# Two record scatters in every chunk of the attention, in a kernel of pooled attention and a noisy top-2 mixture of experts

## The chip, the cores and the metric

One Trainium2 chip, one of its cores. The metric is the device time of one execution in microseconds (us); the kernel before takes 1044.02 us, the median of 3 runs (1043.8 to 1044.55).

The engines are named as in the profile: PE multiplies matrices (PEld is its weight load), DVE works on vectors, ACT evaluates functions, POOL is the general engine that here issues all indirect DMAs, SP issues the plain ones.

## The reference

```python
# attention: q, k, v of 8 batches x 8 heads x 576 tokens x 64
k_p, v_p = mean of k, v over groups of 8 tokens             # 72 pooled keys
attn = softmax(q @ k_p.T / 8)
x = (attn @ v_p) as 4608 tokens x 512
# mixture of 8 experts, 512 -> 1024 -> 512
noisy = x @ w_gate + log1p(exp(x @ w_noise)) * noise
top2 of noisy; weights = softmax over the two
out[token] = sum over its two experts of weight * (relu(x @ w1[e]) @ w2[e])
```

## The kernel before, in words

The attention is cut into four pairs of batches (pr 0 to 3), and a pair into nine chunks of 128 tokens (ci 0 to 8): four units of kind D give two chunks each (jj 0 and 1), one unit of kind R gives a single one, at ci 4. So there are 36 chunks, numbered i = 9 pr + ci. A chunk runs through the letters of an order string: "0", "1" and "2" are the scores (`qk`) of a third of the heads of the next unit, with the exponentials on ACT; "e" transposes a chunk's exponentials; "v" is the product with the pooled values (`av`, of the chunk before), whose division by the row sums DVE writes to xr (L419); "b" runs background work, "x" calls `adv`.

The gate's logits come out of `av` too. When all nine chunks of a pair have them, `route` works out for the pair's 1152 tokens the two experts, the weights and the place in each expert's list. It is a generator, and `advance(n, m)` takes n of its steps in each chunk at "x". Its first steps add up the logits over the heads, for pairs 0 and 1 on POOL (L509, L510), first for eight chunks and then for the last one; DVE goes on from there (L517). Its last steps build a record of four 32-bit words for each token and expert (rec, last word at L635) and put 18 closures on the list `scq`: one indirect DMA each that scatters 128 records to their places in rec_dram (L638). Behind those of pair 1 they put the load of the first group's records (`load_recs`, L679) and its row gathers (`fetch`, L706); behind those of pair 2 the same for the second group; behind those of pair 3 for the third group and for all other experts.

The second argument m of `advance` says how many entries of `scq` are issued then. They are in POOL's queue in that order, and a scatter also waits (pace) for an instruction of the attention of its moment: at "0", "1" and "2" for the last exponential, at "x" for the last product of DVE. `quiet` is 0 in the first chunk of pairs 1 and 2 and the last chunk of pair 1, and 1 elsewhere in the pairs that have something to issue. What is left on `scq` after the last chunk is issued in the first stage of the MoE, by `hook1` with the numbers of POPS for each of the eight steps f, and by `hook` in its second stage.

The MoE takes the rows of each expert in three groups of tiles of 128 rows. Expert 0's first group (4 tiles) is gathered in the attention, and its transposes (L756) stand in the last two chunks. Group by group PE runs stage 1 (L1017: 8 x 12 matmuls) and stage 2 (L1128, 24 matmuls a tile; L1094 where three tiles are joined). The transposes of the second group (2 tiles) stand in PE's order behind the second tile of the first group's stage 2, those of the third (4 tiles) behind the first tile of the second group's. Groups of the other experts come by row gathers (L715) and a copy through DRAM by SP (L720, L723).

Of the kernel before, what the change touches and what calls it, by code (L numbers as in the profile page):

```python
# [19 lines left out]
def kernel(  # L20
# [25 lines left out]
    NP = B // 2  # L46
    NCH = 9
# [92 lines left out]
    STEPS = (2, 2, 2, 2)  # L140
# [193 lines left out]
    def qtr(u, half, hp=None):  # L334
        kind, pr, b, jp = u
        if half == 0:
            QTT[u] = ap_.tile([P, H, P], F32, tag="qT", name=f"qT{pr}_{b}_{jp}", bufs=2)
        elif kind == "R":
            return
        qT = QTT[u]  # L340
        qp = ps2.tile([P, 4, P], F32, tag="one", name=f"qp{pr}_{b}_{jp}_{half}", bufs=2)
        for i in range(4):
            if kind == "R":
                src = QR[pr][:, 2 * i:2 * i + 2]
            else:
                src = QT[b][:, half * 4 + i, 2 * jp:2 * jp + 2]
            nc.tensor.transpose(qp[:, i], src.rearrange("p a d -> p (a d)"), ident)  # L347
        with tc.high_priority(offset=HP if hp is None else hp):
            nc.scalar.copy(qT[:, half * 4:half * 4 + 4], qp)
# [35 lines left out]
    def et(u, jj):  # L385
        kind, pr, b, jp = u
        nm = f"{pr}_{b}_{jp}_{jj}"
        ex = EX[u][:, jj]
        eT = ap_.tile([P, NEB, P], F32, tag="eT", name=f"eT{nm}", bufs=2)
        for n0, n1 in EG:  # L390
            ep = ps2.tile([P, 512], F32, tag="one", name=f"ep{nm}_{n0}", bufs=2)
            for n in range(n0, n1):
                nc.tensor.transpose(ep[:BST, (n - n0) * P:(n - n0 + 1) * P], ex[:, ES[n]:ES[n] + BST], ident)  # L393
            with tc.high_priority(offset=HP):
                (nc.vector.tensor_copy if n0 and EV >> jj & 1 else nc.scalar.copy)(eT[:BST, n0:n1].rearrange("p n t -> p (n t)"), ep[:BST, :(n1 - n0) * P])  # L395
        return eT
# [50 lines left out]
    def wload():  # L447
        if not pieces:
            return
        e, i, h = pieces.pop(0)  # L450
        st = wp.tile([P, DF], F32, tag="wst", name=f"wst{e}_{i}_{h}", bufs=WS)
        if i < 2:
            src = moe_w1[e].rearrange("(p c) f -> p c f", p=P)[:, 2 * i + h]
            dst = st
        else:
            r0 = (i - 2) * 4 * P + h * 2 * P
            src = moe_w2[e, r0:r0 + 2 * P, :].rearrange("(c p) f -> p c f", p=P)
            dst = st.rearrange("p (c f) -> p c f", c=2)
        nc.sync.dma_start(dst, src)
        staged.append(st)  # L460
# [26 lines left out]
    def drain(g):  # L487
        for _ in g:
            pass
# [255 lines left out]
    def rows_of(grp, psum):  # L745
        e, t0, nt = grp
        xh = wp.tile([P, NDB, 4 * P], F32R, tag="q", name=f"xh{e}_{t0}", bufs=2)
        xl = wp.tile([P, NDB, 4 * P], F32R, tag="q", name=f"xl{e}_{t0}", bufs=2)
        XT[grp] = (xh, xl)
        for t in range(nt):  # L750
            xg = XG.pop((e, t0 + t))
            if e == 0:
                xp = psum(f"xp{t0 + t}").rearrange("p (b c) -> p b c", b=NDB)
                xv = xg.rearrange("p (c b) -> p b c", b=NDB)
                for db in range(NDB):
                    nc.tensor.transpose(xp[:, db], xv[:, db], ident)  # L756
                nr = 2 if t0 + t == 9 else 4
                xT = xp.rearrange("p b (r j) -> p b r j", j=32)[:, :, :nr]
            else:
                nr = 2 if t0 + t == 9 else 4  # L760
                xt = pools[0].tile([P, 4, NDB, 32], F32, tag="xt", name=f"xt{e}_{t0 + t}", bufs=2)
                nc.vector.transpose(xt[:, :nr], xg[:, :nr * P].rearrange("p (r i b) -> p r b i", i=32, b=NDB))
                xT = xt.rearrange("p r b j -> p b r j")[:, :, :nr]
            cs = slice(t * P, t * P + nr * 32)
            xhv = xh[:, :, cs].rearrange("p b (r j) -> p b r j", j=32)
            xlv = xl[:, :, cs].rearrange("p b (r j) -> p b r j", j=32)
            SP_[0] = (nc.scalar.copy(xhv, xT), nc.vector.tensor_sub(xlv, xT, xhv.bitcast(F32)))  # L767
            yield
# [13 lines left out]
    def advance(n, m):  # L782
        for _ in range(n):
            while gens:
                try:
                    next(gens[0])
                    break
                except StopIteration:
                    gens.pop(0)
        for _ in range(min(m, len(scq))):  # L790
            scq.pop(0)()
# [84 lines left out]
    for i, (ui, u, jj) in enumerate(chunks):  # L876
        pr, ci = divmod(i, NCH)
        if ci == 0:
            lgs[pr] = (rp if pr % 2 else ap_).tile([P, NCH, H, 2 * E], F32, tag="lg", name=f"lg{pr}")
        single = u[0] == "R"  # L880
        has = ui + 1 < NU
        if single:
            order = OR
        else:
            order = OD[jj]
        eT = None
        quiet = 0 if ci == 0 and pr <= NP // 2 or ci == NCH - 1 and pr < NP // 2 else 1

        def bgs():
            for f in bg.get(i, ()):  # L890
                f()

        def adv():
            pace[0] = lastx[0]
            advance(STEPS[pr], 2 * quiet if pr >= NP // 2 else quiet)

        for o in order + ("" if "b" in order else "b") + ("" if "x" in order else "x"):
            if o == "v" and i == 0:
                drain(pg[0])
            if o == "b":  # L900
                bgs()
            elif o == "x":
                adv()
            elif o == "e":
                eT = et(u, jj)
            elif o == "v":
                if due:
                    due.pop()()
                if ci == NCH - 1 and pr < NP - 1:
                    gens.append(route(pr, 0, NCH, lgs[pr], one))  # L910
                elif ci == NCH - 1:
                    rt = route(pr, 0, NCH, lgs[pr], lambda nm: mone(nm))
                    next(rt)
                due.append(lambda u=u, jj=jj, ci=ci, eT=eT, lg=lgs[pr]: av(u, jj, ci, eT, lg))
            elif o in "012":
                if has:
                    qk(units[ui + 1], int(o))
                    if pr and (o == "0" or not single):
                        pace[0] = lasta[0]
                        advance(0, quiet)  # L920
            elif ui + 2 < NU:
                qtr(units[ui + 2], "qr".index(o))
        if i == 24:
            for _ in range(WS):
                wload()
        if i == 33:
            splits = rows_of(groups[0], one)
        if pr == 3 and ci:
            with tc.issue_after(lastl[0].ins), tc.issue_after(lasta[0].ins):
                next(first[0], None) if ci < 5 else next(first[1], None)  # L930
        if ci == 4 and pr >= HS:
            gens.append(route(pr, 0, 5, lgs[pr], one))
# [206 lines left out]
    def mone(name):  # L1139
        return bank()  # L1140
# [10 lines left out]
                    wgens.pop(0)  # L1151

    s0 = SP_[0]
    POPS = {0: (8, 0, 0, 2, 3, 3, 3, 3), 1: (100, 0, 0, 0, 0, 0, 0, 0)}

    def hook1(i, f):
        if i == 0 and f == 0:
# [2 lines left out]
        elif i == 0:  # L1160
            next(rt, None)
            next(rt, None)
        advance(0, POPS[i][f])

# [151 lines left out]
```

## Time and profile before

| what | value |
|---|---|
| median of 3 runs | 1044.02 us |
| span of the profiled execution (its own time, from its first to its last instruction) | 1041.8 us |
| PE busy | 995.3 us, 96% |
| POOL busy | 371.0 us, 36% |
| record scatters, L638 | 72, 76.2 us |

The span is that of one execution taken by the hardware profiler. Busy times are shares of that span; an engine that is idle costs time only where the end of the program waits for it. The profile shows the granted clock of PE (PEclk, as a share of full speed) by stretches.

### The profile page before, as it was taken

The numbers are of one execution on the slowest core, as the hardware profiler recorded it, in microseconds if no ns is written. First come the engines' busy times: TensorE is split into PE (matmuls) and PEld (weight loads), VectorE is DVE, ScalarE is ACT, GpSimd is POOL, SyncE is SP. The second block draws the span as 40 slices with busy tenths as digits, with TensorE's granted clock in tenths as the row PEclk, the third lists the DMA queues.
The fourth block names the chain that finished last, engine by engine and source line by source line (L and its number), as shares of the span: only waits on it lengthen the run. The fifth ranks groups of instructions, "written<-read, shape, count | busy, mean of one in ns | idle before, by whom it ended". The sixth has DMA issues, their size and how long they took to land.

```text
span 1041.8 us, 16452 instructions
## 1 busy us (share of the span) xinstructions
PE 995.3 (96%) x5832; PEld 889.2 (85%) x5832; DVE 549.0 (53%) x1277; ACT 345.5 (33%) x857; POOL 371.0 (36%) x419
## 2 busy tenths in 40 slices
PE   7998989699999999999999999999999999999996
PEld 5897878587998898888988898889888988898995
DVE  5798768494343554554445445444554455456242
ACT  5786667541123122321232123212321232124120
POOL 4024462537310433154215421542154215421514
PEclk9999989799999999999999999999999999999999
DMA  9997853244615656577348736773577357844624
GB/s 277 336 305 235 274 155 103 82 138 118 181 60 144 211 191 191 144 242 219 111 131 249 233 120 170 249 227 100 151 248 245 116 142 258 249 137 142 203 88 136
DMA packets 137382, 190.36 MB, mean 183 GB/s; under 512 B 29155, under 2 KB 84084, under 8 KB 137274
## 3 DMA queue, kind: packets, MB, share of 16 engines
q1 hardware_dynamic: 111834, 121.84, 38.8%
q0 software_dynamic: 25440, 67.05, 20.6%
q8 instruction: 72, 1.18, 0.5%
q14 instruction: 36, 0.29, 0.1%
HBM read 126.07 MB, written 70.74 MB: 189 GB/s over the span
## 4 chain that ended last, share of the span: by engine, by line
PE 88%; issue 3%; ACT 2%; DVE 1%; DMA 1%; POOL 1%; another core or an unknown queue 1%; SPq 1%; POOLq 0%; DVEq 0%; ACTq 0%
PE bank L1017 37%; PE bank L1128 27%; PE bank L1094 10%; PE a L408 5%; PE s L375 3%; PE ep L393 2%; PE qp L347 2%; ACT ex L382 1%; DMA v<-in_v_dram 1%; ACT eT L395 1%; POOL out_dram L1073 1%; PE kT L298 0%; PE vr L325 0%; SPq L219 0%
## 5 line engine op out<-in xcount | busy, mean ns | idle before, releaser
L1017 PE MATMUL bank<-xh,w 128*128 128x512 f32 (+6 forms) x1536 | 390.4, 338 | 0.6 <-issue 0.6
L1017 PEld LDWEIGHTS bank<-xh,w 128*128 128x128 f32 x1536 | 270.3, 188 | 21.4 <-issue 0.9
L1128 PE MATMUL bank<-w,hh 128*128 128x512 f32 x880 | 271.7, 390 | 1.3 <-issue 1.2
L1017 PE MATMUL bank<-xl,w 128*128 128x512 f32 (+6 forms) x768 | 259.7, 338 | 1.2 <-issue 0.9
L1028 ACT ACTIVATE hh<-bank 128x512 fp32r<-128x512 f32 (+4 forms) x192 | 96.7, 510 | 459.9 <-PE bank L1017 369.2
L1029 DVE SCALAR_TENSOR_TENSOR hl<-bank,hh 128x512 fp32r<-128x512 f32 (+4 forms) x192 | 110.1, 579 | 243.1 <-ACT hh L1028 212.7
L1128 PEld LDWEIGHTS bank<-w,hh 128*128 128x128 f32 x880 | 164.8, 188 | 34.8 <-issue 1.1
L1128 PE MATMUL bank<-w,hl 128*128 128x512 f32 x440 | 171.4, 390 | 1.0 <-issue 1.0
L1017 PEld LDWEIGHTS bank<-xl,w 128*128 128x128 f32 x768 | 144.6, 188 | 11.3 <-DVE xl L767 0.6
L1065 DVE SCALAR_TENSOR_TENSOR pv<-bank,raw,pv 128x128 f32<-128x128 f32 x196 | 55.5, 342 | 111.8 <-DMA pv<-slot_dram,raw 51.8
L1069 POOL DMA_DIRECT2D slot_dram<-yt x17 | 9.8, 576 | 276.0 <-DVE yt L1065 225.5
L638 POOL DMA_INDIRECT rec_dram<-rec,pos x72 | 76.2, 1058 | 85.3 <-DVE rec L635 26.9
L1094 PE MATMUL bank<-hh,w 128*128 128x240 f32 (+3 forms) x512 | 103.6, 298 | 2.2 <-issue 1.7
L1128 PEld LDWEIGHTS bank<-w,hl 128*128 128x128 f32 x440 | 82.6, 188 | 19.5 <-issue 2.4
L1049 POOL DMA_INDIRECT pv<-slot_dram,raw x70 | 68.7, 982 | 62.4 <-DMA slot_dram<-ys 34.2
L481 DVE TENSOR_TENSOR w<-wst,w 128x512 fp32r<-128x512 f32 x128 | 82.6, 682 | 11.1 <-ACT w L480 10.6
L1094 PEld LDWEIGHTS bank<-hh,w 128*128 128x128 f32 x512 | 82.6, 189 | 2.7 <-issue 2.1
L480 ACT CAST w<-wst 128x512 fp32r<-128x512 f32 x128 | 73.0, 618 | 27.1 <-DMA wst<-in_moe_w_dram 27.1
L715 POOL DMA_INDIRECT row<-x_dram,raw x70 | 70.2, 1004 | 21.3 <-issue 20.7
L1069 POOL DMA_DIRECT2D slot_dram<-pv x55 | 31.7, 576 | 125.1 <-DVE pv L1065 89.2
L1094 PE MATMUL bank<-hl,w 128*128 128x320 f32 (+3 forms) x256 | 76.0, 297 | 0.0
L382 ACT ACTIVATE ex<-s,mx 128x72 f32<-128x72 f32 x288 | 70.8, 342 | 12.8 <-DVE mx L380 7.5
(165 smaller groups left out, 1032.3 us busy)
## 6 DMA issues: line engine op xcount, KB each, us to landing
wst<-in_moe_w_dram SPq DMA_DIRECT2D x64, 512.0 KB
via<-row SPq DMA_DIRECT2D x266, 64.0 KB
xg<-via SPq DMA_DIRECT2D x63, 256.0 KB
slot_dram<-pv POOLq DMA_DIRECT2D x55, 256.0 KB
k<-in_k_dram SPq DMA_DIRECT2D x7, 1280.0 KB
v<-in_v_dram SPq DMA_DIRECT2D x16, 512.0 KB
x_dram<-xr SPq DMA_DIRECT2D x16, 512.0 KB
q<-in_q_dram SPq DMA_DIRECT2D x7, 1024.0 KB
```

Source lines behind the costliest of these rows:

```text
L382: lasta[0] = nc.scalar.activation(ex[:, jj, EPOS[h] * G:(EPOS[h] + 1) * G], sv[:, i], AF.Exp, bias=mx[:, i:i + 1])
L480: nc.scalar.copy(hv, sv)
L481: nc.vector.tensor_sub(lv, sv, hv.bitcast(F32))
L638: s = nc.gpsimd.indirect_dma_start(out=rec_dram[:, :], out_offset=bass.IndirectOffsetOnAxis(ap=pos[:, i, c:c + 1], axis=0), in_=rec[:, c, ...
L715: turn_of("pool", lambda: nc.gpsimd.indirect_dma_start(out=row[:32 * nr], out_offset=None, in_=x_dram[:, :], in_offset=bass.IndirectOffset ...
L1017: nc.tensor.matmul(part(ph), w1s(e, a, db, f), part(xs[b][:, db]), start=(i == 0), stop=(i == 3 * NDB - 1))
L1028: act = nc.scalar.activation(hh[:, :n], ph[:, :n], AF.Relu)
L1029: last = nc.vector.scalar_tensor_tensor(hl[:, :n], ph[:, :n], 0.0, hh[:, :n].bitcast(F32), op0=OP.max, op1=OP.subtract)
L1049: turn_of("pool", lambda: nc.gpsimd.indirect_dma_start(out=pv[:np_], out_offset=None, in_=slot_dram[:P + e * CAP, :], in_offset=bass.Indir ...
L1065: nc.vector.scalar_tensor_tensor(r_, y_, wc, pv[:plain] if plain else r_, op0=OP.mult, op1=OP.add)
L1094: nc.tensor.matmul(part(py), w2s(e, b, f)[:, mb * P:(mb + 1) * P], part(hs[f][a]), start=(i == 0), stop=(i == 3 * NFB - 1))
L1128: mm = nc.tensor.matmul(py, hs[f][a][:, cs], w2s(e, b, f), start=(i == 0), stop=(i == 3 * NFB - 1))
```

## The change

The number of entries of `scq` issued in a chunk no longer depends on the pair or on `quiet`, which goes away. From pair 1 on, one is issued behind the first scores of a chunk (at "0" for the first chunk of a unit and the single one, at "2" for the second chunk of a unit), and in every chunk one at "x". Nothing is issued at "1". The last two chunks have no scores of a next unit and issue only the one at "x". At the first step of the MoE all that is left is issued (100 in place of 8).

```diff
-        quiet = 0 if ci == 0 and pr <= NP // 2 or ci == NCH - 1 and pr < NP // 2 else 1
-
         def bgs():
             for f in bg.get(i, ()):
                 f()
 
         def adv():
             pace[0] = lastx[0]
-            advance(STEPS[pr], 2 * quiet if pr >= NP // 2 else quiet)
+            advance(STEPS[pr], 1)
...
-                    if pr and (o == "0" or not single):
+                    if pr and (o == "0" or o == "2" and not single):
                         pace[0] = lasta[0]
-                        advance(0, quiet)
+                        advance(0, 1)
...
-    POPS = {0: (8, 0, 0, 2, 3, 3, 3, 3), 1: (100, 0, 0, 0, 0, 0, 0, 0)}
+    POPS = {0: (100, 0, 0, 2, 3, 3, 3, 3), 1: (100, 0, 0, 0, 0, 0, 0, 0)}
```

## Rows read from the trace of the kernel before

**Rows 1.** The page: busy time of each engine; the group of the scatters.

```profile
PE 995.3 (96%) x5832; PEld 889.2 (85%) x5832; DVE 549.0 (53%) x1277; ACT 345.5 (33%) x857; POOL 371.0 (36%) x419
...
L638 POOL DMA_INDIRECT rec_dram<-rec,pos x72 | 76.2, 1058 | 85.3 <-DVE rec L635 26.9
```

**Rows 2.** Stretches: length, busy us of PE, PEld, DVE, ACT, POOL (instructions), PEclk, DMA.

```profile
88.54:102.49 13.95, 11.32 (x86) 9.69 (x84) 10.18 (x20) 9.74 (x33) 9.92 (x9) 1.00 0.71 177
102.49:115.23 12.74, 12.72 (x99) 12.28 (x100) 10.32 (x27) 9.79 (x33) 6.03 (x8) 0.87 0.77 236
115.23:124.74 9.51, 8.24 (x85) 7.39 (x80) 6.97 (x27) 7.01 (x26) 5.39 (x5) 1.00 0.91 312
124.74:135.35 10.61, 10.00 (x90) 8.08 (x88) 8.69 (x44) 6.34 (x23) 2.29 (x4) 1.00 0.66 208
135.35:161.81 26.46, 22.09 (x140) 20.27 (x141) 15.68 (x35) 15.97 (x54) 19.51 (x18) 0.81 0.45 131
161.81:186.22 24.41, 22.11 (x199) 18.74 (x198) 20.46 (x90) 18.16 (x62) 4.74 (x6) 1.00 0.39 131
186.22:204.21 17.99, 7.66 (x57) 7.07 (x56) 5.21 (x15) 7.31 (x26) 11.71 (x12) 0.74 0.18 46
204.21:213.59 9.38, 8.72 (x49) 8.07 (x48) 7.80 (x19) 4.63 (x9) 4.75 (x6) 0.78 0.57 155
```

**Rows 3.** The chain of waits in order of time: start, length, what.

```profile
195.22 7.78 another core or an unknown queue
```

**Rows 4.** POOL in order of time: start, length, instruction [idle before, releaser].

```profile
135.21 0.97 POOL L638 DMA_INDIRECT rec_dram<-rec,pos  x1 [7.71 <-DVE rec L635]
...
161.11 0.97 POOL L638 DMA_INDIRECT rec_dram<-rec,pos  x1 [0.30 <-issue]
163.49 0.59 POOL L679 DMA_DIRECT2D raw<-rec_dram  x1 [1.42 <-DMA rec_dram<-rec,pos]
...
186.52 1.00 POOL L638 DMA_INDIRECT rec_dram<-rec,pos  x1 [15.79 <-DVE rec L635]
...
200.62 0.96 POOL L638 DMA_INDIRECT rec_dram<-rec,pos  x1 [0.30 <-issue]
```

**Rows 5.** PE and ACT in order of time, near the longest holes.

```profile
194.64 0.42 PE L393 MATMUL ep<-ident,ex 128*112 128x128 f32 x1 [2.50 <-remote]
...
203.03 0.59 ACT L395 COPY eT<-ep 112x512 f32<-112x512 f32 x1 [7.80 <-remote]
...
203.66 1.98 PE L756 MATMUL xp<-ident,xg 128*128 128x128 f32 x8 [7.83 <-ACT eT L395]
```

**Rows 6.** POOL and DVE in order of time, route of pair 1 and chunk 30.

```profile
112.75 0.89 POOL L509 TENSOR_TENSOR lg<-lg 128x64 f32<-128x64 f32 x2 [0.40 <-DVE lg L421]
...
113.98 0.23 DVE L517 SCALAR_TENSOR_TENSOR rt<-rt 128x72 f32<-128x72 f32 x1 [0.47 <-POOL rt L510]
...
177.09 0.68 DVE L419 TENSOR_TENSOR xr<-a,rd 128x512 f32<-128x512 f32 x1
```

**Rows 7.** POOL and SP in order of time, a row gather and its copy.

```profile
271.54 1.01 POOL L715 DMA_INDIRECT row<-x_dram,raw  x1 [0.31 <-issue]
...
274.99 8.24 SPq L720 DMA_DIRECT2D via<-row  x16
```

**Rows 8.** POOL in order of time, at the start of the MoE.

```profile
223.31 0.58 POOL L679 DMA_DIRECT2D raw<-rec_dram  x1 [1.42 <-DMA rec_dram<-rec,pos]
226.93 1.36 POOL L706 DMA_INDIRECT xg<-x_dram,raw  x1 [3.04 <-DMA raw<-rec_dram]
...
233.00 1.18 POOL L638 DMA_INDIRECT rec_dram<-rec,pos  x1 [3.44 <-DVE rec L635]
...
262.17 1.01 POOL L706 DMA_INDIRECT xg<-x_dram,raw  x1 [4.31 <-DMA raw<-rec_dram]
```

**Rows 9.** The chain of waits in order of time, the MoE's first groups.

```profile
245.99 0.96 PE bank L756 x8
...
278.01 1.92 PE bank L756 x16
```

## The prediction

> **What bounds the kernel now.** I read the page first: PE is busy for 96% of the span and POOL, which issues the 72 record scatters (76.2 us), for 36% [rows 1]. So POOL's own time buys nothing, and the question is where PE is not busy. Outside the attention there is hardly such a place, so the second view is the table of stretches from the first record scatter to the first MoE matmul [rows 2]. The reader is to see two kinds of stretch in it. In three of them POOL issues scatters back to back (88.54 to 102.49, 135.35 to 161.81, 186.22 to 204.21: 58.40 us together), and PE is idle for 2.63 + 4.37 + 10.33 = 17.33 us, 29.7%. In the other five (66.65 us) PE is idle for 0.02 + 1.27 + 0.61 + 2.30 + 0.66 = 4.86 us, 7.3%. The longest single hole is in the chain too: 7.78 us from 195.22 whose releaser the profile can't name [rows 3]. Third, POOL in order of time says why the scatters lie so [rows 4]: the route of pair 1 was to hand its records out from chunk 21 on, but its record words come from DVE only at 135.2, by when several chunks' worth is queued; a scatter takes 0.97 us and the next can follow 0.30 us later, and all 18 go in one run, the last at 161.11. Pair 2's start at 186.52 after a wait of 15.79 us and run on to 200.62. Fourth, PE's idle time in the third run: 2.50 us before 194.64, without a releaser, and 7.83 us before 203.66, put down to an ACT copy that itself had waited 7.80 us for something unnamed [rows 5]. No row names a scatter as the cause; only the coincidence does.
>
> **The change part by part.** The profiled execution has a span of 1041.8 us and the median of the runs is 1044.02, so 2.2 us lie around the span; I make the sum on the span and add them.
>
> *The scatters themselves.* 72 before, 72 after; no instruction is added on PE, DVE or ACT. Counting pops: before, a chunk of pair 1 takes 2 or 3, of pairs 2 and 3 takes 3 or 4, and chunks 17 and 18 none. After, each takes 2 (the last two chunks 1 each). Pair 0's scatters then end in chunk 21 in place of 20, pair 1's in chunk 30 in place of 26, and of pair 2's 18 only 7 are issued in the attention in place of 16.
>
> *What spreading buys.* The nearest rows for a chunk with two scatters are 115.23 to 124.74 (5 in 9.51 us) and 204.21 to 213.59 (4 in 9.38 us): idle 1.27 + 0.66 = 1.93 us of 18.89, 10.2% [rows 2]. PE's busy time in the eight stretches is 102.86 us. At 10.2% idle throughout they take 102.86 / 0.898 = 114.5 us in place of 125.05: 10.5 us less. Not all runs go: a route that comes late still finds pops waiting, 5 for pair 0 (chunks 12 to 14), 5 for pair 1 (chunks 21 to 23), about 3 for pair 2, so 13 x 1.27 = 16.5 us stay dense, and at 29.7 - 10.2 = 19.5% that is 3.2 us. I take 10.5 - 3.2 = 7.3 us. The ends are 0 (the idle time has another cause, for which speaks that the 10.33 us of the third stretch are two holes that no row ties to POOL) and 10.5.
>
> By the Trainium skill ("DMA: Bandwidth & Descriptors", Specifications) a DMA write under 512 bytes is a read-modify-write, a cost that goes with the number of pieces and not with their spacing. A record here is 16 bytes and the number stays, so by that rule this term would be 0; the trace's 29.7 against 10.2% speaks for spacing, without proving it. That is the first rival below.
>
> *Route 1's adds on POOL.* Chunks 17 and 18 now have scatters between the two groups of adds. The second group starts at 112.75, and DVE's next route step waited for it until 113.98 [rows 6]. After it, a scatter at the end of chunk 17 and one behind the scores of chunk 18 precede it: 2 x 1.27 = 2.5 us, less the 0.4 us that POOL waits there. DVE is in order, so the weights of the next block, the reciprocal and the output product are queued behind that step, and PE waits for the first. Between 0 and 2.1 us; I take 1.0, since part lies beside matmuls of scores that need only earlier DVE work.
>
> *Load and gathers for the first MoE group.* The load follows the last scatter of pair 1 by 2.4 us (163.49 against 161.11 [rows 4]), a first gather its load by 3.6 us (226.93 against 223.31 [rows 8]). That scatter moves to chunk 30, in which DVE's product stands at 177.09 [rows 6], so the load comes at 179.5 and four gathers from 183.1 to 186.9, one each 1.27 us as with scatters. A gather's rows are there about 3.4 us after its issue (the first row gather at 271.54, the copy that needs it at 274.99 [rows 7]): 190.3. The transposes that need them are at 203.66 [rows 5], or near 195 if the holes go. Cost 0, cover some 5 us; without it each us late is a us of PE.
>
> *The first MoE stage.* Eleven scatters of pair 2 in place of two stand ahead of the load and the two gathers of group 1, and behind them on POOL the 18 scatters of pair 3, two slot writes and the gathers of group 2. Nine more at 1.27 us: 11.4 us. Load 223.31 becomes 234.7, first gather 226.93 becomes 238.4, the second 239.7, rows there at 243.1 [rows 8]. PE transposes them at 245.99 [rows 9]: covered by 2.9 us. But the nine land while the weight loads of expert 0 run, and the load waits for them; the wait of 1.42 us before 223.31 was without such loads. So 0 to 4 us; I take 0.5. Pair 3's run from 233.00 starts at 241.4, 8.4 us later; its gathers at 262.17 move to 270.6, the fourth is issued at 274.4 and there at 277.8. PE transposes at 278.01 [rows 9]: 0 to 3 us; I take 0.5.
>
> Sum: -7.3 + 1.0 + 0 + 0.5 + 0.5 = -5.3 us. Span 1036.5, time 1038.7 us.
>
> **The rivals.** *The idle time has nothing to do with the scatters' spacing.* For it: no scatter is named as releaser in rows 5; ACT and PE both stand still from 195.83 to 203 while POOL goes on as usual to 200.62. Against it: three of three dense stretches have it, and none of the five others more than 14%. Then the gain is 0 and the covers hold: +0 to +2, time about 1045.0.
>
> *POOL's queue at the start of the MoE becomes the bound.* Place: the transposes of group 1 at 245.99. PE is in order, so it stands until the second gather's rows are there. It decides from a delay of 2.9 us beyond the 11.4 worked out, which eleven scatters that land slowly beside weight loads can give; past that each us costs one, and group 2 follows, since pair 3's records wait behind group 1's gathers on POOL and come later by as much. Price 4 + 3 us with 1 to 2 us of the adds; with half of the gain or none of it in the attention the time is 1044.02 + 8 - 4 = 1048 (1046.1 to 1052). Against it: the 2.9 us of cover, and the raw load is small.
>
> *All of the holes go,* the remaining runs too: -10.5 + 1.0, time 1034.5.
>
> *The change doesn't do what it says* in part: since records come late, bursts stay; that is in the 3.2 us.
>
> **How the numbers follow.** My forecast has 0.38 (its own range 1035.5 to 1041.9), all holes gone 0.09, no tie to the spacing 0.21, POOL's queue 0.32. What a measurement of this kernel can tell from no change is 0.2%, 2.1 us: 1041.9 to 1046.1. Faster: 0.38 + 0.09 = 0.47, and 0.01 from the middle rival: 0.48. Same: 0.20. Slower: 0.32. The range goes from 1033.5, below the case with all holes gone, to 1049.5, where the POOL rival's upper part is left out.
>
> **What would show it.** Right: in the trace after, the scatters of chunks 25 to 30 come in twos with gaps of some us, PE's idle time from 135 to 204 falls from 17 us to under 10, no hole of over 2 us is left, and the load of group 1's records stands near 235 counted as now. Wrong: a hole of some us stands in the same place of the attention with only two scatters near it (first rival), or PE waits at the transposes of groups 1 or 2 for a gather (second rival), or DVE waits for POOL's second add by over 2 us.

## The result, and the profile after

The changed kernel took 1033.5 us (median of 14 runs, 1029.5 to 1038.6), the kernel before beside it 1043.0 (14 runs, 1036.7 to 1049.0): ratio 0.991 [0.989, 0.994]. The forecast was 1038.7. The profiled execution has a span of 1030.1 us against 1041.8.

That is one half of the result. In three later groups of runs, on three chips, the same kernel before took 1006.5 to 1007.5 us; on one of them the changed kernel ran beside it again and was **slower**: 1017.4 against 1007.5 us, ratio 1.0085 [1.0057, 1.0112]. Both signs have to be explained. I call the first comparison A and the repeat B; on which chip A ran is not recorded.

The instructions of PE, DVE, ACT and SP and their order are the same in both kernels. On POOL the differences of order are two scatters ahead of route 1's second adds and three memsets a few places earlier; all else is the moment from which a scatter may go.

The page of the changed kernel in A, beside [rows 1]: in these lines little moves but POOL's wait for the records, 26.9 us before.

```profile
PE 992.9 (96%) x5832; PEld 888.0 (86%) x5832; DVE 550.2 (53%) x1277; ACT 343.8 (33%) x857; POOL 375.3 (36%) x419
...
L638 POOL DMA_INDIRECT rec_dram<-rec,pos x72 | 76.8, 1066 | 76.6 <-DVE rd L415 18.6
```

The stretches of [rows 2], after, in A; the ends are the same products of the same chunks (length, busy us of PE, PEld, DVE, ACT, POOL, PEclk, DMA). The last line goes on to 300 us.

```profile
89.72:101.49 11.77, 10.53 (x82) 9.30 (x81) 10.06 (x20) 9.43 (x33) 8.44 (x8) 1.00 0.63 146
101.49:116.35 14.86, 12.47 (x111) 11.70 (x110) 11.44 (x27) 10.49 (x38) 9.93 (x12) 1.00 0.92 301
116.35:124.40 8.05, 6.74 (x69) 6.13 (x69) 6.98 (x27) 5.88 (x22) 4.44 (x4) 1.00 0.79 280
124.40:135.00 10.60, 10.29 (x93) 8.54 (x92) 8.69 (x43) 6.27 (x24) 1.31 (x3) 1.00 0.66 209
135.00:153.86 18.86, 17.79 (x140) 16.47 (x141) 15.59 (x35) 15.71 (x55) 12.06 (x11) 1.00 0.62 183
153.86:179.60 25.74, 22.68 (x203) 19.23 (x201) 20.50 (x91) 17.65 (x61) 12.34 (x13) 1.00 0.39 119
179.60:187.64 8.04, 7.81 (x49) 7.32 (x48) 5.20 (x14) 6.94 (x26) 4.13 (x5) 0.79 0.38 109
187.64:196.09 8.45, 7.34 (x50) 6.55 (x51) 7.79 (x19) 4.91 (x11) 4.56 (x6) 1.00 0.63 196
196.09:300.00 103.91, 95.96 (x498) 84.66 (x497) 48.62 (x150) 25.88 (x54) 46.87 (x49) 0.95 0.43 117
```

Two things are to be seen. The three stretches that held the dense runs fall from 58.40 us [rows 2] to 11.77 + 18.86 + 8.04 = 38.67, and the whole attention from 125.05 to 106.37. The second stretch, with route 1's adds, grows from 12.74 to 14.86. And behind the attention the kernel loses: from the last product to the end it is 1041.8 - 213.59 = 828.2 us before and 1030.1 - 196.09 = 834.0 after.

The places that the prediction named, after, in A: POOL's pair 1, its load and gather [rows 4], the load and gather of group 1 and the gather of group 2 [rows 8].

```profile
134.87 0.97 POOL L638 DMA_INDIRECT rec_dram<-rec,pos  x1 [8.99 <-DVE rec L635]
...
166.55 1.06 POOL L638 DMA_INDIRECT rec_dram<-rec,pos  x1 [0.93 <-ACT ex L382]
169.81 0.59 POOL L679 DMA_DIRECT2D raw<-rec_dram  x1 [2.19 <-DMA rec_dram<-rec,pos]
172.70 1.07 POOL L706 DMA_INDIRECT xg<-x_dram,raw  x1 [2.30 <-DMA raw<-rec_dram]
...
219.80 0.58 POOL L679 DMA_DIRECT2D raw<-rec_dram  x1 [3.56 <-DMA rec_dram<-rec,pos]
222.59 2.14 POOL L706 DMA_INDIRECT xg<-x_dram,raw  x1 [2.22 <-DMA raw<-rec_dram]
...
254.47 1.01 POOL L706 DMA_INDIRECT xg<-x_dram,raw  x1 [3.88 <-DMA raw<-rec_dram]
```

DVE's route step behind the second adds, where it waited 0.47 us before [rows 6]; then PE's longest waits from 88 to 196 us and from 196 to 330 us (total, times, longest), where [rows 3, 5] had a hole of 7.8 us:

```profile
115.10 0.23 DVE L517 SCALAR_TENSOR_TENSOR rt<-rt 128x72 f32<-128x72 f32 x1 [2.78 <-POOL rt L510]
```

```profile
PE ep L393 <- ACT ex L382: 2.7, 2, 1.4
PE vTp L317 <- ACT eT L395: 1.3, 1, 1.3
...
PE bank L1015 <- issue: 6.7, 7, 1.8
```

No hole of over 1.4 us is left in the attention. The 6.7 us without a releaser are late in pair 3's run of 18 scatters, in the stage of group 1.

### The profile page after: what moved, and what is told of

Same layout as the page of the kernel before. It is cut to its first block, busy times and chain, and to the rows that moved or that the text cites. A ratio compares the mean times of both kernels' runs of the same rounds, so it can differ in the third digit from the quotient of the medians.

```text
span 1030.1 us, 16456 instructions
## 1 busy us (share of the span) xinstructions
PE 992.9 (96%) x5832; PEld 888.0 (86%) x5832; DVE 550.2 (53%) x1277; ACT 343.8 (33%) x857; POOL 375.3 (36%) x419
## 4 chain that ended last, share of the span: by engine, by line
PE 89%; issue 3%; DVE 2%; POOL 2%; ACT 2%; DMA 1%; SPq 0%; another core or an unknown queue 0%; POOLq 0%; ACTq 0%; DVEq 0%
PE bank L1015 38%; PE bank L1126 27%; PE bank L1092 10%; PE a L408 4%; PE s L375 3%; PE ep L393 2%; PE qp L347 2%; DMA q<-in_q_dram 1%; ACT ex L382 1%; POOL out_dram L1071 1%; PE kT L298 0%; POOL lg L509 0%; ACT eT L395 0%; PE s L365 0%; PE vr L325 0%
## 5 line engine op out<-in xcount | busy, mean ns | idle before, releaser
L715 POOL DMA_INDIRECT row<-x_dram,raw x70 | 76.0, 1086 | 21.4 <-issue 20.1
```

Of the source, the lines that this page charges most:

```text
L715: turn_of("pool", lambda: nc.gpsimd.indirect_dma_start(out=row[:32 * nr], out_offset=None, in_=x_dram[:, :], in_offset=bass.IndirectOffset ...
```

## The experiments

"The attention" below is the time from the product of chunk 13 to that of chunk 35, the stretches of [rows 2].

**No scatters.** The kernel before, and the changed one, with each scatter left out (the table of records is not filled, the rest runs).

```
-                scq.append(lambda c=c, i=i: scatter(c, i))
+                scq.append(lambda: None)
```

> The kernel before with all 72 record scatters left out, so the later loads read the padding records; every other instruction stays, in the same order. Theory (runs of scatters, one directly behind the other on POOL, hold PE up): the holes go; from the first to the last product of the attention (DVE, L419) 165 to 169 us in place of 186.6 before and 167.9 after, and the time falls below that of the kernel after, to 1016 to 1026 us. Rival (the holes have another cause, such as instruction fetch or the loads of q, k and v, and went for a reason of timing): holes of 2 us and more stay, 175 us or more, time over 1033.

> The kernel after with all 72 record scatters left out. Theory: the same time as the kernel before without scatters, within 0.3%, since the change moves nothing but scatters: 1016 to 1026 us, so that the scatters still cost the kernel after 8 to 17 us. Rival (the gain came from something else that the change moved, the later load and gathers of the first group among them): it differs from the kernel before without scatters by 5 us or more.

Measured, beside a kernel before of 1006.5 us: 1005.3 (ratio 0.9986 [0.9965, 1.0008]) and 1006.3 (1.0005 [0.9970, 1.0040]). Without scatters the two kernels are not told apart. But with all 72 the kernel before was as fast there, so on this chip no hold-up was left to be explained; both expectations (1016 to 1026 us) had taken A's level for granted, and missed.

**Dense on purpose.** The changed kernel with 18 scatters at once at the ends of chunks 14, 25 and 33.

```
-            advance(STEPS[pr], 1)
+            advance(STEPS[pr], {14: 18, 25: 18, 30: 1, 31: 1, 33: 18}.get(i, 0))
-                        advance(0, 1)
+                        advance(0, 0)
```

> The kernel after, but the 18 scatters of each of pairs 0, 1 and 2 are handed to POOL at once (at the end of chunks 14, 25 and 33); the loads and gathers behind them keep their chunks. PE, DVE, ACT and SP keep their order. Theory: three runs of 18 in the attention bring holes back; the attention takes 180 us or more and the time is 1040 to 1056 us. Rival (it is not the runs): within 0.3% of the kernel after, 1030 to 1037, or less, since nothing is left over for the first MoE stage.

Measured: 1025.2 us, ratio 1.0194 [1.0165, 1.0224] to the kernel before there (the changed kernel was not run beside it). That is slower, as the spacing theory says, though less than its 1040 to 1056 us (which took A's level for granted), and for another reason. PE's waits from 88 to 260 us, POOL behind the first run, and the second run's stretch:

```profile
PE ep L393 <- ACT ex L382: 8.1, 1, 8.1
PE xp L756 <- DMA xg<-x_dram,raw: 2.8, 2, 1.6
```

```profile
117.16 0.97 POOL L638 DMA_INDIRECT rec_dram<-rec,pos  x1 [0.30 <-issue]
118.16 2.06 POOL L509 TENSOR_TENSOR lg<-lg 128x512 f32<-128x512 f32 x2
```

```profile
154.00:180.00 26.00, 25.40 (x232) 22.90 (x232) 24.52 (x92) 20.95 (x71) 19.91 (x18) 1.00 0.35 106
```

The first run has a hole of 8.1 us because route 1's adds stand behind all 18 scatters on POOL and begin only at 118.16. The 2.8 us are two waits for the gathers of group 0, which here stand behind the second run and just ahead of the third. The second, with 18 scatters in 26 us and nobody waiting for POOL, leaves PE busy for 25.40 of 26.00 us at full clock: dense, and no hold-up.

**More DMAs of POOL in the MoE.** The changed kernel with 18 more per expert: scatters, gathers or plain writes that nobody reads.

```
+        if joined(g) and e in EXTRA:
+            for k in range(18):
+                extra(k, EXTRA[e])
```

> The kernel after with 18 more small DMAs of POOL added per expert, which nobody reads and which wait for nothing: experts 1 and 4 scatters of 128 records of 16 bytes to DRAM, experts 2 and 5 gathers of 128 such records from DRAM, experts 3 and 6 plain writes of 128 such records. They stand where PE streams matmuls and POOL is idle for some 30 us. Theory in its general form (any run of small POOL DMAs holds PE up): PE holes put down to issue, 1 us and more each, late in the runs of all three kinds. Theory for scatters alone: holes in experts 1 and 4 and none in the others, 2 to 10 us each. Rival: no hole that was not there (the kernel after has one of 2.4 us behind a branch near 398 us).

Measured: 1074.4 us, one run. It decides nothing on the three kinds: the planner, which orders POOL's instructions, set them in front of real gathers, and PE's long waits (two, 41.0 us together, for ACT, which waited for rows) were again POOL's queue.

**The same two kernels again.** Unchanged, one after the other on one chip: comparison B.

> The kernel before, unchanged, for its trace beside the others. Spacing theory (a run of scatters issued back to back holds PE up): the attention's products span some 185 us and PE has holes of some us in the runs 140 to 151 and 190 to 204, wherever it runs. Chip theory (the holes belong to the chip or the launch and not to the scatters' spacing): where the time is near 1006 us, as on the second chip, the products span near 157 us and no hole of over 2 us is in them, though the two runs of scatters stand in the same places.

> The changed kernel, unchanged. Spacing theory: 8 to 10 us faster than the kernel before, on every chip. Chip theory: where the kernel before takes about 1006 us there are no holes to win back, so only the wait for route 1's adds on POOL is left (2.78 against 0.47 us): 0 to 4 us slower than the kernel before; where the kernel before takes about 1043 us, 8 to 10 us faster.

Measured: 1007.4 and 1017.4 us (ratio to all runs of before there 1.0085 [1.0057, 1.0112]). For the kernel before, the chip theory came out; for the changed one both missed (the chip theory allowed 0 to 4 us). The stretches of [rows 2] in the kernel before, in B:

```profile
88.31:98.94 10.63, 9.96 (x81) 9.16 (x80) 10.15 (x20) 9.39 (x33) 8.50 (x8) 1.00 0.60 149
98.94:110.47 11.53, 11.52 (x105) 11.06 (x104) 10.32 (x28) 9.83 (x34) 8.33 (x10) 1.00 1.04 314
110.47:118.19 7.72, 7.72 (x83) 7.18 (x78) 6.96 (x27) 6.85 (x26) 5.40 (x5) 1.00 1.04 361
118.19:128.51 10.32, 10.01 (x91) 8.25 (x89) 8.70 (x44) 6.24 (x23) 2.29 (x4) 1.00 0.80 257
128.51:145.57 17.06, 17.06 (x140) 16.38 (x141) 15.36 (x35) 15.51 (x55) 13.71 (x12) 1.00 0.68 203
145.57:167.95 22.38, 21.79 (x200) 18.74 (x199) 20.42 (x90) 17.91 (x62) 12.20 (x12) 1.00 0.35 115
167.95:174.63 6.68, 6.52 (x54) 6.22 (x52) 5.15 (x14) 6.68 (x25) 5.16 (x5) 1.00 0.68 195
174.63:182.56 7.93, 7.12 (x50) 6.47 (x51) 7.76 (x19) 4.88 (x11) 6.10 (x7) 1.00 0.65 207
```

94.25 us in place of 125.05, with the same instructions. Ahead of the first scatter the two executions agree: from the first product to that of chunk 12 it is 56.72 us in A and 56.73 in B.

```profile
27.02:83.74 56.72, 56.12 (x493) 50.07 (x494) 47.74 (x128) 42.47 (x143) 5.45 (x6) 1.00 1.00 327
```

```profile
26.77:83.50 56.73, 56.13 (x493) 50.07 (x494) 47.71 (x127) 42.48 (x143) 5.46 (x6) 1.00 0.99 329
```

So A's excess begins where the scatters begin. In the stretches of the three dense runs it is 3.32 + 9.40 + 11.31 = 24.03 us, in the other five 6.77. For the changed kernel the excess of A over B in the attention is 8.12 us.

It does not end with the scatters. Behind the attention the kernel before takes 6.9 us more in A (828.2 against 1003.9 - 182.56 = 821.3). One and the same matmul (L1017) starts at 285.42 in A and at 251.26 in B, 34.16 us apart, against 31.03 at the last product of the attention; so 3.1 us lie around pair 3's run of scatters and 3.7 behind it, where no record is scattered. From 300 us on, PE's waits without a releaser in A are these:

```profile
PE bank L1094 <- issue: 1.7, 3, 1.1
PE bank L1017 <- issue: 1.5, 3, 0.9
```

The longest of each, before 407.38 and before 612.54, follow runs of six gathers on POOL (the last at 405.30 and 610.26). So in A holes come behind dense gathers too, again by coincidence only. And in A's longest hole, from 196 to 203.9 us, the DMA engines move 160 packets, all of the five scatters issued there: no load of data or of program code was under way for which PE or ACT could have waited.

The changed kernel in B, where it differs in the attention, and the stage behind it:

```profile
100.47:115.30 14.83, 12.56 (x111) 11.78 (x110) 11.30 (x27) 10.56 (x38) 9.81 (x12) 0.99 0.98 303
115.30:123.78 8.48, 8.48 (x72) 7.89 (x72) 6.93 (x27) 6.14 (x22) 4.44 (x4) 0.81 0.84 290
...
188.08:290.00 101.92, 98.11 (x516) 86.43 (x516) 51.99 (x154) 27.64 (x55) 45.86 (x49) 0.97 0.43 120
```

The first two are 3.30 and 0.76 us longer than in the kernel before; the other six agree within 0.06 us. The waits of PE there, in full:

```profile
PE bank L756 <- DMA xg<-x_dram,raw: 3.8, 6, 1.0
PE ep L393 <- ACT ex L382: 1.3, 1, 1.3
PE ep L393 <- ACT eT L395: 1.0, 1, 1.0
```

The 1.3 and 1.0 us stand behind route 1's adds (DVE waits 2.79 us for POOL there), and the granted clock of 0.81 in the 8.48 us behind them is worth some 0.19 x 8.48 = 1.6 us: 3.9 of the 4.06. The 3.8 us are waits for gathers: 0.96 and 0.24 at the two tiles of group 1, and 0.20, 0.72, 0.78 and 0.92 at the four of group 2, of which these are the last three:

```profile
252.73 0.74 PE L756 MATMUL bank<-ident,xg 128*128 128x128 f32 x4 [0.72 <-DMA xg<-x_dram,raw]
254.26 0.75 PE L756 MATMUL bank<-ident,xg 128*128 128x128 f32 x4 [0.78 <-DMA xg<-x_dram,raw]
255.92 1.13 PE L756 MATMUL bank<-ident,xg 128*128 128x128 f32 x4 [0.92 <-DMA xg<-x_dram,raw]
```

A clock of 0.97 over 101.92 us is worth some 3.1 us, together 6.9 against 6.1 measured (1015.5 - 188.08 against 1003.9 - 182.56).

**One part alone.** First, in the changed kernel, twos as in the change, but the chunks around a block's end stay without scatters; second, in the kernel before, these chunks opened, but three or four a chunk as before.

```
+        quiet = 0 if ci == 0 and pr <= NP // 2 or ci == NCH - 1 and pr < NP // 2 else 1
-            advance(STEPS[pr], 1)
+            advance(STEPS[pr], quiet)
-                        advance(0, 1)
+                        advance(0, quiet)
```

```
-        quiet = 0 if ci == 0 and pr <= NP // 2 or ci == NCH - 1 and pr < NP // 2 else 1
+        quiet = 1
```

> One part alone: two scatters a chunk as in the changed kernel, but the chunks around the end of a block stay without any, as before (17 and 18 among them), so route 1's adds meet no scatter on POOL. Spacing theory: the gain of the changed kernel and up to 2 us more. Theory that the early scatters of chunks 17 and 18 make the gain (POOL starts to hand out earlier, so less is left for the later runs): less than half of the changed kernel's gain. Chip theory with no holes: within 1 us of the kernel before, and 0 to 4 us faster than the changed kernel.

> The other part alone: the chunks around the end of a block are opened to scatters as in the changed kernel, but pairs 2 and 3 keep their three or four scatters a chunk, so the dense runs stay. Spacing theory: no gain, and the wait for route 1's adds: 0 to 3 us slower than the kernel before. Theory that the early start makes the gain: most of the changed kernel's gain. Chip theory with no holes: as the changed kernel, 0 to 4 us slower than before.

Measured in B: 1035.1 (ratio 1.0259 [1.0235, 1.0283]) and 1014.3 us (1.0059 [1.0037, 1.0082]). PE's longest waits of the first kernel and of the second:

```profile
PE xp L756 <- DMA xg<-x_dram,raw: 11.1, 2, 10.8
PE bank L756 <- DMA xg<-x_dram,raw: 8.6, 5, 5.5
```

```profile
PE ep L393 <- ACT ex L382: 4.6, 1, 4.6
```

The first missed by 27 us against what every theory had said. With chunks 17 and 18 empty and only two a chunk after them, pair 1's last scatter comes so late that the load of group 0 is issued at 182.53 in place of 168.60 in the changed kernel (both in B), and PE stands 10.8 us at its first transposes: the cover that the prediction counted on, used up. (Twelve matmuls of one chunk and a few steps of DVE change places in it too.) The second has more scatters ahead of the second adds, and DVE waits 4.85 us in place of 2.79.

**Each queue by itself.** The changed kernel with chunks 17 and 18 empty and three a chunk behind them; with three a chunk in the last nine chunks; with both.

```
+        quiet = ci == NCH - 1 and pr == NP // 2 - 1 or ci == 0 and pr == NP // 2
+            advance(STEPS[pr], 0 if quiet else 2 if pr == NP // 2 else 1)
...
+                        advance(0, 0 if quiet else 1)
```

```
+            advance(STEPS[pr], 2 if pr == NP - 1 else 1)
```

> The changed kernel, but chunks 17 and 18 stay without scatters, so that route 1's adds on POOL come first, and chunks 19 to 26 take three to make up for them. Queue theory (the change costs only where POOL's queue makes somebody late, at route 1's adds and at the gathers of the MoE groups): the holes of 1.0 and 1.3 us and the half clock around 110 to 118 us go, 4 us of the attention; the gathers stay late. On a chip where the kernel before takes some 1007 us: about 1013.4, 4 us under the changed kernel, 6 us over the kernel before. Hold-up theory alone (only the spacing of the scatters decides): no change against the changed kernel, 1017.

> The changed kernel, but the last nine chunks hand out three scatters each as before, so that fewer of pair 2's are left for the MoE stage. Queue theory: the transposes of groups 1 and 2 wait for no gather (3.8 us in the changed kernel) and the half clock behind them goes; the wait for route 1's adds stays: about 1011.5 on a chip where the kernel before takes 1007. Hold-up theory alone: at or over the changed kernel's 1017.

> Both edits at once: no scatters in chunks 17 and 18, three a chunk from there on. Queue theory: within 2 us of the kernel before where that takes 1007 us, with no hole of over 0.7 us between 88 and 300 us. Hold-up theory alone: slower than the changed kernel.

Measured, beside a kernel before of 1007.0 us: 1011.9 (ratio 1.0050 [1.0017, 1.0084]), 1010.7 (1.0039 [1.0019, 1.0059]) and 1007.0 (0.9992 [0.9975, 1.0010]). The longest waits of PE from 88 to 300 us, in this order:

```profile
PE bank L756 <- DMA xg<-x_dram,raw: 3.0, 3, 1.6
```

```profile
PE ep L393 <- ACT ex L382: 1.3, 1, 1.3
PE ep L393 <- ACT eT L395: 1.0, 1, 1.0
```

```profile
PE xp L756 <- ACT eT L395: 0.6, 2, 0.3
```

Each edit takes its own wait away and leaves the other's; with both, the longest is 0.3 us. The queue theory's numbers (6, 4.5 and within 2 us over the kernel before) came out as 4.9, 3.7 and 0.0.

**Scatters that nobody waits for.** The kernel before with 12 more, handed out where POOL would wait for pair 2's records.

```
             scq.append(lambda: fetch(groups[0]))
+            for k in range(12):
+                scq.append(lambda k=k: idle(k))
```

> The kernel before, and 12 more scatters of pair 1's records into a table that nobody reads, handed out in chunks 28 to 31 while POOL would wait for pair 2's records: nothing of the kernel depends on them. Chip theory: on a chip where the kernel before takes 1007 us they cost 1 us or less (12 times at most 0.03, from 72 scatters that made no difference there, and a last pair of scatters that moves by 2.5 us); on one where it takes 1043 us 12 times 0.2 to 0.9, 2 to 10 us. Hold-up theory (a dense run always holds PE up): 5 us or more on every chip.

Measured: 1015.8 us, ratio 1.0076 [1.0047, 1.0106], more than the chip theory allowed. The number is one that the hold-up theory allows (5 us or more), but the time is not lost where the scatters are. The attention and PE's longest wait:

```profile
95.03:189.33 94.30, 91.76 (x787) 83.55 (x786) 84.97 (x270) 77.16 (x261) 64.69 (x61) 1.00 0.69 209
```

```profile
PE bank L771 <- DMA xg<-x_dram,raw: 5.4, 3, 4.0
```

The attention takes 94.30 us with the 12 against 94.25 without (in B): beside the matmuls they cost nothing that can be told. But they take turns that pair 2's scatters had, so the load of group 1 goes at 217.28 and its transposes wait 4.0 us; from the last product to the end it is 1017.4 - 189.33 = 828.1 us against 821.3. I had counted the scatters and not the turns that they take. (The profiled execution, the longest of the six, also lost 6.7 us before the product of chunk 13, where nothing of the edit stands: 95.03 against 88.31.)

## Why the prediction was right or wrong

**What bounds the kernel.** Right for A that PE's holes stand where scatters come densely, and that this is a coincidence that no row explains. Against B it is more: the excess of A is nothing ahead of the first scatter and, in the attention, 24.03 of 30.80 us in the three dense stretches. But outside the attention, where the prediction saw hardly a place, A lost 6.9 us too, 3.7 of them where no records are scattered.

**What spreading buys (-7.3, bounds 0 and -10.5).** The step's direction held in A and its size didn't. The attention fell by 18.7 us; with the adds taken out (2.1 us by the growth of their stretch in A, 4.0 by B) the gain is 20.8 to 22.7, three times the forecast and twice its bound. The floor was wrong: I took the 10.2% of idle time beside single scatters for the kernel's own, and PE's 102.86 busy us as given. In B the same stretches are busy for 91.7 us and idle for 2.7%: in A the busy time too held lost clock (0.74 to 0.87 in four of the eight stretches of [rows 2], 1.00 in all of B's). What the prediction would look for came: from 135.00 to 187.64 PE is idle for 4.4 us, and no hole of 2 us is left.

**Route 1's adds (+1.0, 0 to 2.1).** The mechanism was the one described, the size too small. DVE waits 2.78 us, 2.3 more and over the 2 us that the prediction had named as a sign of being wrong; the stretch grew by 2.1 us in A and 3.3 in B. In B the clock behind it fell to 0.81, 4.0 us in all (in A it stayed at 1.00 there). The clock was no term of the sum.

**Load and gathers of group 0 (0).** Right: load at 169.81, gathers from 172.70, and no wait at their transposes. The cover is real, and small: 14 us later it cost 10.8.

**First MoE stage (0.5 + 0.5).** This is the step that failed: measured 5.8 us in A and 6.1 in B. Its first half was near: eleven scatters delay the load in A by 14.0 us counted from the last product (219.80 - 196.09 against 223.31 - 213.59; 11.4 was forecast), the first gather in B by 12.5, and in B PE waits 1.2 us at group 1. The second half was far off: in B, at group 2, PE consumes four tiles in 0.75 us each while POOL issues a gather each 1.27 us, so it waits at several in turn, and then runs at half the clock (granted 0.50 from 255.1 to 261.8). In A the wait is not at the gathers: PE had been held earlier, by holes without a releaser in pair 3's run, 6.7 us of them.

**The rivals.** That the holes have nothing to do with the spacing: in A nothing but the scatters' moments changed and three quarters of the excess in the attention went, which speaks against it without showing how; in B there are no holes to ask about. That POOL's queue at the start of the MoE takes the gain back was priced at 4 + 3 us with 1 to 2 of adds, against 6.1 and 4.0 in B, and it is the whole effect there: slower by 9.9 us. It lost in A because the gain was three times the forecast. In A both are there: -18.7 in the attention (spreading and adds together), +5.8 behind it, and +1.2 before the first scatter (where nothing of the change lies) make the -11.7 of the span.

**The time.** 1033.5 us lies below the forecast's own range (1035.5 to 1041.9), below even the case with all holes gone (1034.5), and just inside the whole range. The sign is owed to A's holes, for on the later chip the same change is slower; that the sum came so near is luck, since a gain too small by 13 us or more and costs too small by 6 to 8 (2.0 forecast, 5.8 behind the attention and 2.1 to 4.0 at the adds) partly cancel.

By the Trainium skill ("DMA: Bandwidth & Descriptors", Specifications) a DMA write under 512 bytes is a read-modify-write. The prediction made of it a cost that goes with the number and not with the spacing. On the later chips the runs show neither: spacing is worth nothing that can be told (25.40 of 26.00 us busy in a dense run), and 72 scatters together cost 1.3 us, not told from none. In A the time moved with the spacing. What makes A and B differ stays open, the chip, the launch or something else; A's chip was not met again, and the kernel without scatters was not run there, so that its floor is B's is an inference from the equal stretch ahead of the scatters.

The kernel with both queues mended is not told from the kernel before on a chip where that takes 1007.0 us, and was not measured in A, so no version is shown to beat both.

## What to carry to other kernels

A queue that is shared by bulk work and by work that somebody waits for is costed by the waiting instructions: write down for each of them how many entries now stand ahead of it, times the interval of the queue (1.27 us here), against its cover, and add the lost clock behind each hole. A hole that the profile can't name may belong to the chip or the launch and not to the kernel: run the kernel before on another chip before a change is built on it.

## What was not expected of the hardware

The same kernel took 1043.0 us in one group of runs and 1006.5 to 1007.5 in three others, 3.6% apart, with much the same duration of a scatter (1.06 us on the mean in A [rows 1], 1.09 in B) and the same 56.7 us of attention ahead of the first. In A's worst run the attention lost 0.9 us for each dense scatter (11.31 us for 12), in B nothing that can be told; and A has holes behind dense gathers too. And short holes cost more than their length: 2.3 us of them in B were followed by a granted clock of 0.81 over 8.48 us.
